# A memory attention and channel mix kernel: all steps put in a new order

## The chip, the cores and the metric

The kernel runs on one core of one Trainium2 chip. The time is device microseconds of that core for one execution of the whole program. Before the change it is 191.7 us (median of 3 runs, 191.69 to 191.99).

## The reference

Two layers, cut to what is computed. For each of 8 batches and 8 heads, 576 tokens of width 64 are first gathered into 32 memory slots, then read back; the result is the input `x` (8 x 576 x 512) of a channel mix.

```python
a = exp(phi - max(phi)); a = a / sum(a)          # over the 576 tokens
k_m = einsum('bhsm,bhsd->bhmd', a, k)            # 32 slots of 64
v_m = einsum('bhsm,bhsd->bhmd', a, v)
attn = softmax(q @ k_m.T / 8)                    # 576 x 32
x = (attn @ v_m) as [B, S, 512]

xk = mu_k * x + (1 - mu_k) * x_prev              # x_prev: the token before
xr = mu_r * x + (1 - mu_r) * x_prev
out = sigmoid(xr @ w_r) * (relu(xk @ w_k) ** 2 @ w_v)
```

## The kernel before, in words

All matrix products are in bf16. The work is cut into steps, and the order of the steps is written out by hand in a list of words, PLAN (lines 19 to 84). A loop at the end of the kernel (lines 794 to 807) takes word after word and issues that step's instructions, so the place of a word in PLAN is the place of its instructions in the queue of each engine that it uses. Nothing reorders them later.

```python
for word in " ".join(PLAN).split():
    word, _, used = word.partition("@")
    word, _, now["by"] = word.partition("/")
    now["banks"] = iter(used)
```

A word is read like this. `2:kv@15` is step `kv` of batch 2, with its PSUM tiles in banks 1 and 5. `/a` or `/d` behind a word says that ScalarE (ACT) or VectorE (DVE) makes the copy. A step that has several parts (matmul, copy, matmul again) stands in the list once for each part.

- `p:k:2` (`preload`, lines 195 to 222) issues the load of k of batch 2 on the queue of GpSimd (POOL); `p:wr`, `p:wv`, `p:wk` load pieces of the weights. k, v and q of two batches fit at a time, phi likewise. A load is cast from f32 to bf16 on its way.
- `exp` makes the exponential of phi on ACT, `z` its sum (matmul with a column of ones, line 329), `kv` the products k_m and v_m (72 small matmuls, line 319). For batch 0 k comes in f32 in two halves and is cast by `c00` to `c11`; its products are `kg0`, `kg1`, those of v `vg0`, `vg1`.
- `nk` scales k_m into `kbd` (line 344 on ACT, 346 on DVE), `tk` transposes it (line 368) and copies it to `kmT` (line 372); `q0`, `q1` transpose q on DVE (line 388); `s` makes the scores (32 small matmuls, line 402), `es0`, `es1` their exponentials; `fe`, `fs`, `fo` the denominators on DVE; `w0`, `w1` the weights `atn` (line 465).
- For batches 1 to 7 x is never made. v_m goes through the weights first: `nv`, `vt` transpose v_m, `G` multiplies it with w_k and w_r (line 492), `E` copies the result to `G` in SBUF (line 498), `D` is a difference of two of those (line 501). Then `c2:5` makes block 5 of 8 of the keys of batch 2: a first part (2 matmuls, line 617), a copy of it into a second PSUM bank (line 621), a second part (4 matmuls, line 625). `g:20` does the same for the gates (lines 679, 683, 687). `r` is the relu (line 583 on ACT, 585 on DVE), `s:25` the square (lines 589, 591), `t` the tanh that stands for the sigmoid (line 656).
- For batch 0 x is made by `mk0`, `mk1`, `mr0`, `mr1` (line 362) and unloaded by `u`; `c0:5a` is a key block of its first half of tokens (line 599), `g:00` to `g:03` are its gates (line 666).
- `o:21` multiplies the squares of one tile of 128 tokens with w_v (8 matmuls, line 757), multiplies with the gate on DVE (line 763) and stores. Names with `a` or `b` take only a part of the 512 columns. `g:e0` to `g:e3` and `o:e0` to `o:e3` do the same for the tokens that are left over from two batches; `x` gathers their squares.
- `mu` and `mub` (lines 260 to 274) put mu_k and mu_r on the partitions, by a transpose and by a broadcast matmul; `m:k0`, `m:k1`, `m:r0` (line 278) scale the weights by them.
- `b:2x8` are 2 matmuls on zeros of 8 x 64 columns (`keep_busy`, line 251); `WARM` is the first row of them, ahead of PLAN.

The loads of POOL are issued in order; an issue waits until the load eight places before it has landed, and until its buffer is free.

Of the kernel before, what the change touches and what calls it, by code (L numbers as in the profile page):

```python
# [85 lines left out]
WARM = (10, 8)  # L86

PRE = "after: id: q:0a"
TAIL = ("o:72", "o:71a", "o:71b",)


NJ = 9
# [5 lines left out]
def kernel(  # L98
# [158 lines left out]

    keep_busy(*WARM)

# [579 lines left out]
```

## Time and profile before

| | |
|---|---|
| median of the runs | 191.7 us |
| the profiled execution | 191.42 us, its span 189.6 us |
| PE busy | 183.6 us, 97% of the span |
| DVE busy | 155.7 us, 82% |
| ACT busy | 153.2 us, 81% |
| POOL busy | 29.5 us, 16% |
| matmuls on zeros | 46, 14.1 us busy |
| moved by DMA | 31.92 MB |

The span runs from the first to the last instruction; the time of an execution has 1.8 us around it. A row of the timeline gives the start, the duration, the engine, the line, the operation, what it writes and reads, and how many; a bracket at its end gives the idle time of the engine before it and what ended that. For a load there are two rows: one with the place and time of its issue, one with the time from the issue to the landing. Matmuls are pipelined, so the busy time of one overlaps with the next: a row's busy time is more than it adds to the chain. In the chain of waits a row is start, duration, engine, tile, line and count.

### The profile page before, as it was taken

How to read it: one execution, taken by the hardware profiler on the slowest of the kernel's cores; microseconds unless marked ns; L12 is line 12 of the kernel's file. 1: busy time of each engine (PE TensorE's matmuls, PEld its weight loads, DVE VectorE, ACT ScalarE, POOL GpSimd, SP SyncE). 2: the span in 40 equal slices, each digit the busy share in tenths (PEclk: the TensorE clock that was granted, in tenths of full speed). 3: DMA queues.
4: the chain of work that ended last, by engine and by line, in shares of the span. 5: the costliest groups of instructions: out<-in, count | busy, mean ns of one | idle time of the engine just before them, and what ended most of it. 6: DMA issues, size and time to landing. Idle time of an engine off the chain costs nothing.

```text
span 189.6 us, 6095 instructions
## 1 busy us (share of the span) xinstructions
PE 183.6 (97%) x2482; PEld 103.4 (55%) x2482; DVE 155.7 (82%) x335; ACT 153.2 (81%) x366; POOL 29.5 (16%) x45
## 2 busy tenths in 40 slices
PE   7999999999999999999999999999999999999991
PEld 2534774768645466556555645655545554465450
DVE  2346887989999999998999998998899998885441
ACT  2646899979999989999999789878898779687800
POOL 5843431041040400510042000000000000000000
PEclk9999999999999999999999999999999999999998
DMA  5999999999999999999939995124304222162064
GB/s 191 279 203 206 269 205 203 255 226 232 295 223 267 257 232 252 303 194 246 225 52 258 231 242 139 31 59 96 75 3 102 63 59 56 25 144 55 2 152 124
DMA packets 25756, 31.92 MB, mean 168 GB/s; under 512 B 2168, under 2 KB 20352, under 8 KB 25728
## 3 DMA queue, kind: packets, MB, share of 16 engines
q0 software_dynamic: 17888, 20.32, 58.1%
q1 hardware_dynamic: 6528, 9.18, 18.4%
q10 hardware_dynamic: 1312, 2.03, 3.0%
q8 instruction: 19, 0.31, 0.6%
q14 instruction: 9, 0.07, 0.1%
HBM read 38.28 MB, written 9.44 MB: 252 GB/s over the span
## 4 chain that ended last, share of the span: by engine, by line
PE 91%; DMA 3%; ACT 3%; DVE 1%; issue 0%; ACTq 0%
PE pv L757 34%; PE pk L617 8%; PE pk L625 8%; PE pb L625 7%; PE gps L492 6%; PE pk L599 4%; PE kvps L319 4%; PE pr L687 3%; PE pr L679 3%; PE pb L687 3%; DMA k0f<-in_k_dram 3%; PE idle L254 2%; PE pr L709 2%; PE pr L666 2%; PE scps L402 2%; PE zps L329 1%
## 5 line engine op out<-in xcount | busy, mean ns | idle before, releaser
L757 PE MATMUL pv<-wv,sq 128*128 128x512 bf16 (+3 forms) x296 | 60.6, 351 | 0.1
L757 PEld LDWEIGHTS <-sq 128*128 128x128 bf16 x296 | 27.9, 98 | 24.4 <-issue 2.1
L498 ACT CAST G<-gps 128x512 bf16<-128x512 f32 x65 | 34.2, 605 | 2.8 <-PE gps L492 2.7
L763 DVE SCALAR_TENSOR_TENSOR o<-sg,pv 128x512 f32<-128x512 f32 (+3 forms) x41 | 25.0, 614 | 7.7 <-PE pv L757 6.5
L625 PEld LDWEIGHTS <-G 128*128 128x128 bf16 x224 | 21.4, 97 | 9.4 <-issue 0.4
L583 ACT ACTIVATE rl<-pk 128x288 bf16<-128x288 f32 (+2 forms) x48 | 19.0, 416 | 6.0 <-PE pk L625 4.4
L625 PE MATMUL pb<-diff,G 128*128 128x288 bf16 x112 | 22.9, 286 | 0.0
L625 PE MATMUL pk<-diff,G 128*128 128x288 bf16 x112 | 22.9, 286 | 0.0
L617 PE MATMUL pk<-atn,G 128*128 128x288 bf16 x112 | 20.2, 286 | 0.0
L589 ACT ACTIVATE sq<-rl 128x576 bf16<-128x576 bf16 (+2 forms) x30 | 18.9, 645 | 0.6 <-DVE rl L585 0.5
L591 DVE TENSOR_TENSOR sq<-rl 128x576 bf16<-128x576 bf16 (+2 forms) x42 | 16.8, 413 | 2.5 <-ACT rl L583 1.8
L621 ACT COPY pb<-pk 128x288 f32<-128x288 f32 x39 | 15.8, 421 | 2.6 <-PE pk L617 2.4
L583 ACT ACTIVATE rl<-pb 128x288 bf16<-128x288 f32 x38 | 15.5, 428 | 2.0 <-PE pb L625 1.8
L254 PE MATMUL idle<-zeros 128*128 128x512 bf16 (+3 forms) x46 | 14.1, 411 | 1.3 <-DVE zeros L180 1.0
L465 DVE TENSOR_TENSOR atn<-e,lz 128x576 bf16<-128x576 bf16 (+2 forms) x18 | 11.9, 681 | 2.9 <-ACT lz L437 2.9
L501 DVE TENSOR_TENSOR G<-G 128x1024 bf16<-128x1024 bf16 x21 | 14.1, 677 | 0.1
L617 PEld LDWEIGHTS <-G 128*128 128x128 bf16 x112 | 10.3, 97 | 6.9 <-issue 1.7
L498 DVE CAST G<-gps 128x512 bf16<-128x512 f32 x19 | 12.4, 679 | 1.4 <-PE gps L492 1.4
L656 ACT ACTIVATE sg<-pr 128x512 f32<-128x512 f32 x22 | 13.0, 613 | 0.0
L388 DVE STREAM_TRANSPOSE qT<-q 128x576 uint32<-128x576 uint32 (+2 forms) x16 | 11.8, 757 | 0.0
L585 DVE TENSOR_SCALAR rl<-pk 128x288 bf16<-128x288 f32 (+2 forms) x24 | 10.4, 445 | 1.0 <-PE pk L625 0.9
L174 POOL DMA_DIRECT2D kv<-in_v_dram x7 | 5.2, 749 | 37.2 <-PE kvps L319 23.0
(100 smaller groups left out, 288.0 us busy)
## 6 DMA issues: line engine op xcount, KB each, us to landing
out_dram<-o SPq DMA_DIRECT2D x53, 128.0 KB, 2.4
q<-in_q_dram POOLq DMA_DIRECT2D x7, 576.0 KB, 14.7
ph<-in_phi_dram POOLq DMA_DIRECT2D x7, 576.0 KB, 15.7
kv<-in_k_dram POOLq DMA_DIRECT2D x7, 576.0 KB, 16.1
kv<-in_v_dram POOLq DMA_DIRECT2D x7, 576.0 KB, 17.4
out_dram<-o SPq DMA_DIRECT2D x28, 64.0 KB, 5.2
k0f<-in_k_dram ACTq DMA_DIRECT2D x2, 576.0 KB, 6.0
wv<-in_moe_w_v_dram POOLq DMA_DIRECT2D x2, 512.0 KB, 18.0
```

What stands on the lines that cost most here:

```text
L254: nc.tensor.matmul(ps.rearrange("p (a b) -> p a b", b=64), lhsT=zeros, rhs=zeros[:, :64].unsqueeze(1).to_broadcast([128, blocks, 64]), sta ...
L498: return lambda: copier()(g_tile()[:, v, c, GCOLS[i]], st["gps", v, i][c])
L501: return lambda: nc.vector.tensor_sub(g_tile()[:, 1, :, GCOLS[i]], g_tile()[:, 2, :, GCOLS[i]], g_tile()[:, 0, :, GCOLS[i]])
L583: nc.scalar.activation(rl, ps, AF.Relu, scale=HALF ** 0.5)
L589: nc.scalar.activation(dst, rl, AF.Square)
L591: nc.vector.tensor_mul(dst, rl, rl)
L617: nc.tensor.matmul(pa, lhsT=st["G"][:, 2, c, f], rhs=st["at"][:, c, :NP], start=c == 0, stop=False, skip_group_check=True)
L621: copier()(pb, pa)
L625: nc.tensor.matmul(ps, lhsT=st["G"][:, v, c, f], rhs=st["d"][:, kind, c], start=False, stop=c == 1, skip_group_check=True)
L656: nc.scalar.activation(gated[name], ps, AF.Tanh, scale=0.5)
L757: nc.tensor.matmul(pv[:, cols], lhsT=squares, rhs=wv_sb[:, fi, cols], start=(fi == 0), stop=(fi == NF - 1))
L763: nc.vector.scalar_tensor_tensor(o[:, cols], in0=gated[name][:, cols], scalar=1.0, in1=pv[:, cols], op0=AL.add, op1=AL.mult)
```

## The change

PLAN is written anew, with the same set of steps. The first row of matmuls on zeros is 17 long instead of 10, and there are 23 instead of 36 in the rest. The broadcast and the transpose of mu stand behind the first scores of batch 0 instead of in front of everything. The pieces of w_k are loaded in another order, and so are the loads from batch 1 on: phi, k, q of batch 1 instead of q, phi, k; q, v, phi, k of batch 2 instead of phi, v, k, q; phi, k, v, q of batch 3 instead of phi, v, k, q. Many copies, relus and squares change between ACT and DVE. The last values stand as 70, 72, e3, 73, 71 instead of 70, 73, e3, 72, 71, and the stores of 72 go out on one queue instead of two. "A rule for the fetch of instructions" is part of how the new order was found; no instruction of the kernel stands for it.

The diff, cut to the rows that hold the front, the steps around kv of batches 2 and 6, and the end:

```diff
-    "0:exp0 0:mu@0 0:mub@1 0:mub 0:c01/a 0:c11/d 0:c00/a 0:exp1 b:11x8@6 b:1x7@6 0:z@1 0:z 0:c10/a 0:kg0@23 0:kg1",
-    "0:mu 0:h0/d 0:h1/d b:2x8@6 b:1x7@6 0:tk@0 0:q0 0:tk b:2x8@6 b:1x7@6 0:s0@0123 p:q:0b p:v:0h p:v:0g 0:q1",
-    "p:wk:0-2 p:wk:4-8 p:wk:2-4 0:es10 0:es00 b:3x8@6 0:l10@4 0:l10 0:l00@5 0:l00 0:r10 0:y10 0:s1@6701 0:es11",
...
-    "c0:0b/d c0:7b/d 1:z c0:6b/d c0:1b/a c0:7b/d x:0/d 0:mr1@1456 1:k@37 0:ur11/d 0:ur10/a b:1x6@2 0:mr0@0215 1:nk/a",
-    "1:tk@3 1:tk 0:ur01/a b:1x8@7 b:1x6@6 1:s@3725 m:k0/d 0:ur00/a 1:es0 1:es1 g:02@0 g:01@1 g:03@2 1:fe 1:fs 0:tb",
-    "g:00@3 o:02b@5 1:fo p:v:2 1:w0 o:03b@7 g:03 g:02 o:02b o:03b o:01b@4 m:r0/a 1:v@60 g:00 p:k:2 p:q:2 g:01",
...
-    "c1:5 c1:7 o:02a r:161/d r:151/a r:150/d r:171/a r:160/d 2:z@4 1:G02@67 r:170/a 2:z 1:Gs2@43 2:kv@15 1:E020/a",
-    "p:q:3 1:Es20/a 2:nk/a s:16/d s:17/d 1:E021/d s:15/d 1:Es21/a o:03a@0 2:tk@4 c1:1/d@6 2:nv/a c1:4@7 o:03a c1:1",
-    "c1:4/a@3 r:111/a 2:vt@0 g:11@1 r:110/a c1:4 2:tk 2:q0 p:phi:4 2:q1 g:10@4 2:vt/a 2:s@0526 r:140/a r:141/a 2:es0",
...
+    "0:exp1 0:c00/d 0:c01/d 0:exp0 b:2x8@7 b:1x6@7 0:kg0@01 p:q:0b 0:z@2 0:z 0:c11/d p:v:0g b:3x8@7 p:v:0h",
+    "p:wk:4-8 p:wk:2-4 0:q0 p:wk:0-2 p:phi:1 p:k:1 p:q:1 p:wr:0-4 p:wv:2-4 0:c10/a p:v:1 0:kg1 0:h0/d 0:h1/a b:4x8@7",
+    "0:tk@0 0:tk 0:q1 b:1x8@7 0:s0@0145 0:mub@3 0:mu@2 0:es00 0:mub 0:mu 0:es10 b:2x8@7 0:l10@2 0:l10 0:l00@3 0:l00 0:r00",
+    "0:y00 0:r10 0:y10 0:vg0@60 0:s1@1452 0:es11 0:es01 b:2x8@3 b:1x7@3 0:vg1 b:1x8@3 0:l01@7 0:nk0 0:l01 0:nk1",
...
+    "p:wv:0-2 c0:4a/a p:q:2 c0:6a@1 c0:4a/a c0:2a@0 0:r11 c0:2a/d c0:7a@2 c0:7a/a c0:3a@4 0:y11 0:mk1@0573 c0:0a@2",
+    "c0:7a/a c0:6a/d p:v:2 c0:2a/d 0:uk11/d c0:1a@1 0:uk10/a c0:7b@0 c0:1b@3 c0:3a/a c0:1a/d c0:3a/a 1:exp c0:6a/d",
...
+    "0:ur00/a 1:q1 p:phi:2 1:nk/a 0:mr1@3567 0:ur11/a 1:tk@0 1:q0 1:tk 0:ur10/a b:2x8@1 1:s@0157 c0:4b/d 1:es1 1:es0",
...
+    "1:Gs1@47 1:Es01/a 1:G00@02 1:d p:k:2 1:Es00/a 1:G01@65 o:01a@3 1:E001/d 1:E010/d 1:E011/a 1:E000/a c1:3@1",
...
+    "p:k:3 p:v:3 1:Gs2@01 1:Es21/a 2:z 1:G02@24 1:E020/a 1:Es20/d 1:E021/d 1:D2 2:kv@53 g:10@6 2:nk/a 2:tk@0 2:tk",
+    "g:11@1 2:nv/a s:16/d g:10/a@2 g:11/d@4 2:s@0357 g:10 g:11 s:15/d 2:es0 2:vt@0 s:14/d 2:es1 3:exp t:101 2:fe",
...
+    "6:nk/a 5:Es21/a 6:q0 6:q1 o:40@3 6:tk@0 5:E020/a 6:nv/a c5:1 r:550/a 6:tk 6:s@0172 r:510/a g:50@4 6:es0 6:vt@5",
...
+    "r:740/a g:70@0 c7:6/d@3 t:710 c7:6 s:74/d c7:7/a@1 g:70/d@7 c7:7 r:770/a r:760/a r:720/d g:70 r:771/a s:72/d",
+    "g:e3 s:77/a r:761/d s:76/d x:7/a t:700 o:70@2 o:72@1 o:70 o:72 o:e3@4 o:73@6 o:e3 o:73 o:71a@0 o:71b@1 t:701",
+    "o:71a o:71b",
 ]
 
-WARM = (10, 8)
+WARM = (17, 8)
 
-TAIL = ("o:72", "o:71a", "o:71b",)
+TAIL = ("o:71a", "o:71b",)
```

105 rows, old and new, of the table PLAN are left out of this document.

## The prediction

> **What bounds the kernel now.** I read the page first, then what TensorE (PE) waited for, then the chain of work that ended last, the timeline of PE, and last the loads one by one, each with its issue and its time to landing.
>
> ```profile
> span 189.6 us, 6095 instructions
> PE 183.6 (97%) x2482; PEld 103.4 (55%) x2482; DVE 155.7 (82%) x335; ACT 153.2 (81%) x366; POOL 29.5 (16%) x45
> DMA  5999999999999999999939995124304222162064
> q8 instruction: 19, 0.31, 0.6%
> ```
>
> ```profile
> PE idle L254 <- DVE zeros L180: 1.0, 1, 1.0
> PE zps L329 <- ACT em L299: 0.2, 1, 0.2
> ```
>
> The second fence is the whole list of waits of PE: 1.0 us before its first instruction and 0.2 us at about 8.5 us. So PE is the bound from 8.5 us to its last matmul at 185.45, and its instruction stream has no stall to be won. The DMA digits matter as much: 9 or more until about 95 us, so the loads form a line that is never empty for half of the kernel.
>
> ```profile
> 18.08 3.31 PE L599 MATMUL pk<-x0T,wk 128*128 128x256 bf16 x28
> 30.11 0.48 PE L402 MATMUL scps<-qT,kmT 32*32 32x288 bf16 x32
> 30.52 1.69 PE L666 MATMUL pr<-wr,x0T 128*128 128x512 bf16 x7
> 48.17 0.84 PE L319 MATMUL kvps<-kv,em 64*32 64x128 bf16 x72
> 52.25 0.48 PE L402 MATMUL scps<-qT,kmT 32*32 32x288 bf16 x32
> 185.45 0.35 DVE o L763
> ```
>
> These are my marks of the timeline: the first key matmul of batch 0 (18.08), the scores of batch 1 (1:s, 30.11), the first gate (30.52), kv of batch 2 (2:kv, 48.17), the scores of batch 2 (2:s, 52.25) and, from the chain, the end of PE.
>
> **The change part by part.** The set of steps is the same in both kernels; only order, banks, fillers and the engine of some copies differ. So the forecast is a comparison of when PE comes to the same mark with the same work behind it.
>
> *Fillers and mu.* The matmuls on zeros go from 46 to 40 (17 instead of 10 in the first row).
>
> ```profile
> 5.37 2.96 PE L254 MATMUL idle<-zeros 128*128 128x512 bf16 x12
> 4.75 0.69 PE L263 MATMUL mub<-mu,sel 8*128 8x128 f32 x4
> 8.45 0.78 DVE L304 CAST kv<-k0f 128x576 bf16<-128x576 f32 x1 [2.22 <-DMA k0f<-in_k_dram]
> ```
>
> The second half of k of batch 0 is in at 8.45 in both kernels, and everything before it is cover: the fillers ahead of it (20 instead of 22) cost nothing. With 17+3 of them PE is done at about 7.0 and idles some 1 us until the casts of k are through; nothing waits for that. The mu broadcast (0.69) and the mu transpose move behind the scores of batch 0, where three fillers of about 0.22 each (from the row of 12) stood in before. DVE's copies of them lie beside the exponentials there. I take 0, with 0.3 as the upper end.
>
> *The front, until 1:s.* Both kernels go through one chain of waits there: kv, kbd, kmT, scores, exponential, logarithm, weights, mixed rows, first key matmul. The new order brings kbd on two engines at once, and v's two products ahead of the second scores instead of behind the second denominators. I get the first key matmul at about 17.6 instead of 18.08, and with 3 fillers instead of 5 behind it 1:s near 29.3 instead of 30.11: a lead of about 0.75, an estimate from 17.6 on: 0.5 there and two fillers (0.4, of which the longer batch-1 chain keeps a part). Its ends are 0 and 0.9: the first gate needs w_r, and in the load line w_r keeps its place.
>
> ```profile
> L201 POOL DMA_DIRECT2D wr<-in_moe_w_r_dram x1: 742/742/742, 12.8 to 12.8; - x1
> DMA to landing us min/median/max: 16.8/16.8/16.8
> ```
>
> 12.8 + 16.8 = 29.6, against 30.52 for the first gate before. The lead's size will matter little: the next part ends it in a wait.
>
> *The load line of batch 2.* This decides the forecast. The loads stand on one queue and land in the order of issue. Before, the order behind the last piece of w_v is phi2, v2, k2, q2, phi3, v3, k3; after, it is q2, v2, phi2, k2, phi3, k3, v3.
>
> ```profile
> L201 POOL DMA_DIRECT2D wv<-in_moe_w_v_dram x1: 886/886/886, 18.9 to 18.9; - x1
> DMA to landing us min/median/max: 19.0/19.0/19.0
> ...
> L174 POOL DMA_DIRECT2D kv<-in_k_dram x1: 740/740/740, 24.8 to 24.8; - x1
> DMA to landing us min/median/max: 21.1/21.1/21.1
> ...
> L174 POOL DMA_DIRECT2D q<-in_q_dram x1: 740/740/740, 27.3 to 27.3; - x1
> DMA to landing us min/median/max: 22.8/22.8/22.8
> ...
> L174 POOL DMA_DIRECT2D kv<-in_k_dram x1: 747/747/747, 38.5 to 38.5; - x1
> DMA to landing us min/median/max: 19.8/19.8/19.8
> ```
>
> Landings before: last w_v 18.9 + 19.0 = 37.9; k2 24.8 + 21.1 = 45.9; q2 27.3 + 22.8 = 50.1; k3 38.5 + 19.8 = 58.3. The four loads of batch 2 took 12.2 us in a line that was full. After, the same four loads follow the same piece of w_v, but k2 is the last of them: it lands at about 50.1, where q2 landed, 4.2 us later than before. And 2:kv needs k2.
>
> When does PE come to 2:kv? Before it, the new order has put one half tile of values, one first and two second parts of keys more than the old one:
>
> ```profile
> 42.07 0.87 PE pv L757 x8
> 86.86 0.25 PE pk L617 x2
> 45.53 0.49 PE pk L617 x4
> 51.89 0.43 PE pr L679 x2
> ```
>
> 0.87 + 0.25 + 2 × 0.49 = 2.1 of work brought forward. So PE comes to 2:kv at 48.17 + 2.1 − 0.75 = 49.5, and waits for k2 until 50.1 or later: 0.6 us and more.
>
> Stores share the line. The old order had put out 7 half tiles of batch 0 (128 KB each) by then, the new one has put out the eighth as well. By bytes, 4 loads of 576 KB and 7 × 128 KB went through in 12.2 us, 0.26 MB per us, so one more store is 0.5 us. [...] Without a rule I take 50.35, between 50.1 (the store finds gaps) and 50.6 (it finds none).
>
> *From 2:kv to 2:s.* The old order had enough work behind 2:kv to hide kbd and kmT. The new one has two first parts of gates (0.43 each). What the chain itself needs is seen at batch 1:
>
> ```profile
> 27.73 0.80 PE L319 MATMUL kvps<-kv,em 64*32 64x64 bf16 x72
> 28.61 0.62 ACT L344 ACTIVATE kbd<-kvps,rz 128x128 bf16<-128x128 f32 x2
> 29.28 0.12 PEld L368 LDWEIGHTS <-kbd 128*128 128x128 bf16 x2 [0.27 <-ACT kbd L344]
> 29.72 0.28 DVE L372 COPY kmT<-ktps 128x256 bf16<-128x256 bf16 x1
> 30.11 0.19 PEld L402 LDWEIGHTS <-kmT 32*32 32x32 bf16 x32 [0.60 <-DVE kmT L372]
> ```
>
> From the start of kv to the weights of the scores: 30.11 − 27.73 = 2.4 us. So 2:s starts at 50.35 + 0.05 + 2.4 = 52.8. At 2:s both kernels have the same work behind them, but for one transpose of v (about 0.1) that the new one still owes: even would be 52.25 − 0.1 = 52.15. Loss 0.65. Ends: with k2 at 50.6, 0.9; with k2 no hindrance, PE at 49.5 gives 51.9, a gain of 0.25.
>
> *Batch 3.* 2:kv to 3:kv holds 7.8 of work in the new order, plus about 0.07 for each change between full and split tiles, so 3:kv comes near 59.2. The seven loads up to v3 are the same set as the seven up to k3 before, 58.3: no second stall, but under 1 us of room.
>
> *Batch 6, the same chain.* Between the transposes of k of batch 6 and its scores stands one second part of keys (0.49 and 0.12 for the transposes), and 30.11 − 29.28 = 0.83 is needed: 0.2 lost, ends 0 and 0.4.
>
> *The end.* After the last key matmul ACT now has three relus, a tanh and a square before the first values of batch 7 can finish:
>
> ```profile
> L583 ACT ACTIVATE rl<-pk 128x288 bf16<-128x288 f32 (+2 forms) x48 | 19.0, 416 | 6.0 <-PE pk L625 4.4
> L589 ACT ACTIVATE sq<-rl 128x576 bf16<-128x576 bf16 (+2 forms) x30 | 18.9, 645 | 0.6 <-DVE rl L585 0.5
> L656 ACT ACTIVATE sg<-pr 128x512 f32<-128x512 f32 x22 | 13.0, 613 | 0.0
> ```
>
> 3 × 0.4 + 0.6 + 0.65 = 2.45 against the gate (2 × 0.43) and seven eighths of a tile of values (1.5), together 2.4: with 0.1 to start, 0.1 lost, ends 0 and 0.5.
>
> *Copies moved between ACT and DVE.* By the steps' marks, 4 casts of G and 6 squares net go to DVE, the scalings of w_k and w_r swap engines. At 0.65 and 0.44 that is about 5 us more for DVE: 161 of 177. It hides behind PE as long as the order keeps DVE level; without that cover it is the third rival.
>
> *The fetch of instructions.* 0.31 MB in 19 packets are 16.3 KB each, and 0.6% of the DMA time; no wait of PE is left over for it. [...] I give the rule 0.
>
> **The sum.** Against the profiled execution, 191.42 us (span 189.6 and 1.8 around it): +0.65 at 2:s, +0.2 at 6:s, +0.1 at the end is 0.95, so 192.4. The runs' median, 191.7, stands 0.28 above that execution: 192.6.
>
> **The rivals.**
> *Even.* PE comes to 2:kv and k2 is just there (it lands by 49.6). Then only the chain to 2:s is left: 0.25 gained, 0.3 lost later, 191.75. For it: 2.3 us of room between k2 and 2:kv before; against: the line's sum of bytes.
> *Faster.* The lead of the front gets through whole. That takes k2 landing before 49.2 and kbd and kmT ready at once, since each us of lateness of k2 is one of PE. 191.7 − 0.75, and the two small losses found covered: 191.0. It decides at k2: 49.2. Against it: a line that is 9 or more in every slice.
> *Slower by more.* DVE or ACT falls behind between 40 and 115 us, where the old order had PE busy without a gap. If each of six batches gives 0.3 away, that is 1.8 on top: 194.4. For it: 5 us more on DVE; against: it had 34 us idle.
> *No fetch wait to remove* is part of the forecast.
>
> **How the numbers follow.** Forecast 0.47 (192.1 to 193.2), even 0.22, faster 0.15, slower by more 0.16. A measurement of this kernel tells about 0.2% (0.4 us) from no change. Faster is the rival's 0.15; within 0.2% (191.3 to 192.1) are the even case and a little of the forecast, 0.24; slower is the rest, 0.61. The range leaves out the ends of the outer rivals: 191.1 to 193.8.
>
> **What would show it.** In the new profile PE should have a wait that the old list lacks: kvps of batch 2 on the DMA of k, 0.5 to 1.1 us, near 50; then kbd and kmT before the scores, some 0.5. 1:s should stand near 29.3 and the first gate not before 29.6. k2's landing should be 50.1 to 50.6. If there is no wait at 2:kv, the order of landing was misread; if 3:kv waits too, the stores weigh more than I give them; if waits spread over batches 3 to 6 with DVE or ACT as releaser, the third rival holds.

## The result, and the profile after

The changed kernel takes 193.39 us (median), the kernel before 191.72: a ratio of 1.0068, with a 95% interval of 1.0045 to 1.0091. It is slower by 0.7%. A time given for a kernel is the median of all its executions, while a ratio leaves out those more than 1.5% above the kernel's fastest (here two at 196.5, at a granted clock of 0.982 and 0.991, against 0.994 to 1.0 in the other six). The profiled execution took 193.23 us, its span is 191.2, against 191.42 and 189.6 before: 1.6 more in the span.

The page of the changed kernel, its first lines:

```profile
span 191.2 us, 6061 instructions
PE 181.0 (95%) x2455; PEld 103.1 (54%) x2476; DVE 161.1 (84%) x341; ACT 148.8 (78%) x360; POOL 29.5 (15%) x45
DMA  5999999999999879999639999222314322422064
```

PE is busy for 2.6 us less, 1.2 of it by fewer zeros (part of the rest are records that the trace lacks: it has 21 matmuls fewer than weight loads), and the span is 1.6 longer. The list of all that PE waited for (engine, tile and line, releaser, then the sum, the times and the longest):

```profile
PE idle L254 <- issue: 1.5, 1, 1.5
PE idle L254 <- DVE zeros L180: 1.0, 1, 1.0
PE ktps L368 <- ACT kbd L344: 0.6, 2, 0.3
PE zps L427 <- DVE mu L274: 0.4, 1, 0.4
PE scps L402 <- DVE kmT L372: 0.3, 2, 0.2
PE ktps L368 <- issue: 0.3, 1, 0.3
PE pv L757 <- issue: 0.2, 1, 0.2
```

The wait of kvps on the DMA of k, on which the forecast stood, is not in it. The largest new one is 1.5 us, put down to "issue": PE waited for nothing that the profile shows, and the instruction behind it is a matmul on zeros, which needs no data. The timeline of PE around it, and at the marks of the prediction:

```profile
14.64 0.59 PE L254 MATMUL idle<-zeros 128*128 128x512 bf16 x2
16.76 0.35 PE L254 MATMUL idle<-zeros 128*128 128x448 bf16 x1 [1.52 <-issue]
17.04 0.45 PE L319 MATMUL kvps<-kv,em 64*32 64x64 bf16 x36
...
19.14 2.90 PE L599 MATMUL pk<-x0T,wk 128*128 128x256 bf16 x24
...
30.94 0.55 PE L402 MATMUL scps<-qT,kmT 32*32 32x288 bf16 x29
...
51.09 0.85 PE L319 MATMUL kvps<-kv,em 64*32 64x128 bf16 x72
...
53.43 0.48 PE L402 MATMUL scps<-qT,kmT 32*32 32x288 bf16 x32 [0.17 <-DVE kmT L372]
...
183.09 3.64 PE L757 MATMUL pv<-wv,sq 128*128 128x512 bf16 x24
```

The last row of the kernel before, for the same 24 matmuls:

```profile
181.78 3.64 PE L757 MATMUL pv<-wv,sq 128*128 128x512 bf16 x24
```

So the loss is there at 1:s already (30.94 against 30.11: 0.83), is 1.28 at 2:s (53.43 against the "even" 52.15) and 1.31 at the last values (183.09 against 181.78). Nothing is lost in the 130 us between. Behind PE's last matmuls the changed kernel needs 191.2 − 186.73 = 4.47 us, the one before 189.6 − 185.42 = 4.18: 0.3 more. That makes the 1.6.

### The profile page after: what moved, and what is told of

It reads as the page before. It is cut to its first block, busy times and chain, and to the rows that moved or that the text cites. A ratio compares the mean times of both kernels' runs of the same rounds, so it can differ in the third digit from the quotient of the medians.

```text
span 191.2 us, 6061 instructions
## 1 busy us (share of the span) xinstructions
PE 181.0 (95%) x2455; PEld 103.1 (54%) x2476; DVE 161.1 (84%) x341; ACT 148.8 (78%) x360; POOL 29.5 (15%) x45
## 4 chain that ended last, share of the span: by engine, by line
PE 87%; ACT 7%; issue 2%; DVE 2%
PE pv L757 30%; PE pk L625 8%; PE pb L625 7%; PE pk L617 7%; PE idle L254 6%; PE gps L492 5%; PE pk L599 4%; ACT G L498 3%; PE kvps L319 3%; PE pb L687 3%; PE pr L679 3%; PE pr L687 3%; PE scps L402 2%; PE pr L666 2%; PE pr L709 2%
## 5 line engine op out<-in xcount | busy, mean ns | idle before, releaser
L757 PE MATMUL pv<-wv,sq 128*128 128x512 bf16 (+3 forms) x282 | 59.3, 349 | 0.8 <-issue 0.2
L498 ACT CAST G<-gps 128x512 bf16<-128x512 f32 x61 | 33.0, 612 | 3.6 <-PE gps L492 3.6
L625 PEld LDWEIGHTS <-G 128*128 128x128 bf16 x224 | 21.5, 98 | 9.1 <-issue 0.8
L583 ACT ACTIVATE rl<-pk 128x288 bf16<-128x288 f32 (+2 forms) x41 | 17.0, 422 | 4.2 <-PE pk L625 1.9
L591 DVE TENSOR_TENSOR sq<-rl 128x576 bf16<-128x576 bf16 (+2 forms) x45 | 18.7, 423 | 1.8 <-ACT rl L583 1.1
L621 ACT COPY pb<-pk 128x288 f32<-128x288 f32 x42 | 16.5, 410 | 3.4 <-PE pk L617 2.6
L589 ACT ACTIVATE sq<-rl 128x576 bf16<-128x576 bf16 (+2 forms) x27 | 16.3, 616 | 0.3 <-DVE rl L585 0.2
L498 DVE CAST G<-gps 128x512 bf16<-128x512 f32 x23 | 15.2, 684 | 0.6 <-PE gps L492 0.5
L254 PE MATMUL idle<-zeros 128*128 128x512 bf16 (+2 forms) x40 | 12.9, 438 | 2.6 <-issue 1.5
L585 DVE TENSOR_SCALAR rl<-pk 128x288 bf16<-128x288 f32 (+2 forms) x31 | 13.4, 441 | 1.6 <-ACT sq L589 1.0
L416 ACT ACTIVATE e<-scps 128x288 bf16<-128x288 f32 x28 | 9.2, 419 | 1.8 <-PE scps L402 1.6
```

The lines of the kernel that those rows point to most:

```text
L254: nc.tensor.matmul(ps.rearrange("p (a b) -> p a b", b=64), lhsT=zeros, rhs=zeros[:, :64].unsqueeze(1).to_broadcast([128, blocks, 64]), sta ...
L498: return lambda: copier()(g_tile()[:, v, c, GCOLS[i]], st["gps", v, i][c])
L583: nc.scalar.activation(rl, ps, AF.Relu, scale=HALF ** 0.5)
L585: nc.vector.tensor_scalar(rl, ps, 0.0, HALF ** 0.5, op0=AL.max, op1=AL.mult)
L589: nc.scalar.activation(dst, rl, AF.Square)
L591: nc.vector.tensor_mul(dst, rl, rl)
```

## The experiments

The theory after the result, called the page theory in what was expected: the stall is the wait for PE's own instructions. They come on DMA queue 8. 19 packets of 16.3 KB hold them, and each shows in the trace; what one packet holds is called a page of instructions. Where a kernel's loads fill the DMA queues (a DMA share of 1.25 to 1.32 of the 16 engines from 8 to 20 us in the changed kernel), a packet can come too late. The rivals: some buffer or transfer is late at that place (data theory); the load line of batch 2 decides, as the forecast had it.

Line numbers of most experiments stand one below those of the changed kernel (L253 for L254), in e8_shift eight above. In the view of the DMA queues a stretch of 0.1 us shows a packet (queue, number, MB, share of the 16 engines). The changed kernel, 14.4 to 14.5 us:

```profile
q8 instruction: 1, 0.02, 60.9%
```

The kernel before, 12.8 to 12.9 us:

```profile
q8 instruction: 1, 0.02, 60.1%
```

These are the first packets of the queue in either trace; by their records they start at 14.46 and 12.86. PE stands still from 15.25 to 16.76 in the one and passes without a stop in the other.

**Is it the count of instructions? 14 rows fewer.**

```diff
-WARM = (17, 8)
+WARM = (10, 8)
```

> The changed kernel with 10 instead of 17 wide matmuls on zeros in the first row: 14 TensorE instructions fewer ahead of everything, nothing else. Page theory: queue 8 carries TensorE's instructions in packets of 16 KB (19 packets, 0.31 MB), 256 instructions each, and the stall of 1.5 us at the matmul on zeros ahead of the second half of v's products of batch 0 is the wait for such a packet. Then the stall moves 14 instructions on, into the 36 matmuls of 0:vg1 (which run without a gap in the changed kernel), with 1.0 to 1.6 us, ending near 16.8; the time stays within 0.4 of the changed kernel. Data theory (a buffer, a bank or a transfer is late at that place): the stall stays at the matmul on zeros, or in front of the first matmul of 0:vg1, and never stands between two matmuls of 0:vg1. Zeros theory (the seven fillers themselves cost time): the stall stays and the time falls by up to 1.5.

Measured: 193.31 us, ratio to the kernel before 1.0077 (1.0049 to 1.0105). The stall stands inside 0:vg1, between two of its 36 matmuls that wait for the same data:

```profile
16.34 0.23 PE L318 MATMUL kvps<-kv,em 64*32 64x64 bf16 x6
17.04 0.41 PE L318 MATMUL kvps<-kv,em 64*32 64x64 bf16 x30 [0.47 <-issue]
```

It moved 14 instructions on, as the page theory said, but it is 0.47 long, not 1.0 to 1.6: with ten zeros the granted clock was 0.50 from 7.65 to 11.06 us, and PE came later to the place. The busy time by stretches counts the instructions ahead of the stall (columns: stretch, its length, busy time and count on PE, PEld, DVE, ACT, POOL, granted clock, DMA share, GB/s). The changed kernel, up to its stall:

```profile
0.00:16.70 16.70, 13.32 (x222) 5.87 (x223) 7.04 (x24) 6.73 (x17) 9.94 (x19) 1.00 1.06 222
```

and the one with ten zeros:

```profile
0.00:17.00 17.00, 13.40 (x222) 5.92 (x223) 6.82 (x24) 6.73 (x17) 9.92 (x19) 0.90 1.06 222
```

222 matmuls and 223 weight loads in both: the 446th instruction waits, whichever it is. (The expectations count four records more, which this view leaves out, and call it row 450.) The same 222 and 223 stand ahead of the stall in e4_chain, e6_wk4, e9_mu, e10_tail and e11_vgh below.

**And 158 rows more.** The edit adds 79 small matmuls on zeros as PE's first work, on top of the cut load of e6_wk4 (next):

```diff
+    keep_small(79)      # 64 x 32 tiles, 64 columns
     keep_busy(*WARM)
```

> The changed kernel with w_k's large load cut in two as before, and 79 small matmuls on zeros (64 x 32, 64 columns) as TensorE's first work: 158 rows more ahead of everything. Page theory: the stall in front of 0:vg1 goes, since row 450 is now some 158 rows earlier, at the mu products and zeros behind the first scores (near 12.0), and its packet is asked for at 6 to 7 us; there the stall is 0 to 0.6. The next page begins 256 rows later, between the second scores' denominators and the first key matmuls; asked for near 12.0, with 3.4 us in the line and 2.35 until it is used, it is ready near 17.8: a stall of 0.2 to 1.0 there. 1:s at 29.2 to 29.9, against 29.84 with the cut load alone. Data theory: the stall of 0.3 to 1.5 stays in front of 0:vg1.

Measured: 201.46 us, ratio 1.0485 (1.0402 to 1.0569). The stall ahead of 0:vg1 is gone, and three others are there:

```profile
18.84 0.31 PE L370 MATMUL mxps<-atn,vm 32*64 32x256 bf16 x7 [0.73 <-issue]
...
34.57 0.36 PE L410 MATMUL scps<-qT,kmT 32*32 32x288 bf16 x15 [2.68 <-issue]
...
61.05 0.28 PE L410 MATMUL scps<-qT,kmT 32*32 32x288 bf16 x1 [2.08 <-issue]
```

```profile
0.00:18.80 18.80, 15.36 (x350) 7.28 (x351) 7.95 (x28) 7.53 (x19) 11.41 (x21) 1.00 1.12 223
0.00:34.50 34.50, 27.95 (x606) 16.23 (x607) 19.84 (x63) 19.11 (x48) 16.78 (x28) 1.00 1.18 221
...
32.00:36.00 4.00, 1.38 (x18) 0.60 (x19) 0.84 (x4) 0.99 (x4) 0.74 (x1) 0.93 1.34 202
36.00:40.00 4.00, 4.00 (x13) 1.55 (x12) 3.57 (x5) 2.76 (x6) 0.00 (x0) 0.65 1.25 207
```

701 and 1213 instructions: 445 + 256 and 445 + 3 × 256. (The third stall has 1977 ahead of it in the trace, four short of 445 + 6 × 256.) So by these counts a page is 256 instructions, and 16.3 KB over 256 is 64 bytes each. The place of the first new stall (0.2 to 1.0 in front of the first key matmuls) was expected; 1:s at 29.2 to 29.9 was not met (31.46), and what the shift does further on was not thought of at all. 0.9 us of small matmuls, in a place where PE has only zeros to do, cost 7.2 us by the medians (201.46 against 194.31 with the cut load alone) and 8.35 between the profiled executions (200.6 and 192.25): 5.5 in three stalls, and some 1.7 by a stretch of 3.4 us behind the second one in which the granted clock was 0.50 (35.41 to 38.83). The rest was not traced; 0.78 of it is a wait for the cast of k. The data theory is out.

What a page needs, from all traces: while the loads keep the queues full, its packet mostly starts 2.2 to 3.9 us after PE has begun the page before it, at the front 3.3 to 3.6. From the packet's start to the first instruction behind a stall it took 2.20 to 2.47 us, in eleven stalls of nine kernels. Together about 5.8, an estimate from the middles of the two, 3.45 and 2.34. In the kernel before, 256 instructions of the front last from 9.4 to 15.4, 6.0: it escapes by 0.2. The changed kernel's last from 9.38 to some 15.25, 5.9, but there the packet took 5.1 us to start. The next five kernels ask why.

**One load cut in two.**

```diff
-p:wk:4-8
+p:wk:4-6 p:wk:6-8
```

> The changed kernel with one load cut in two: blocks 4 to 7 of w_k come as two loads of 256 KB (packets of 512 B) instead of one of 512 KB (packets of 1 KB). TensorE's order is the same. In the changed kernel the first packet of queue 8 starts at 14.4, in the kernel before at 12.8, when a load with short packets (w_k, 256 KB) stands in the line. Line theory (the packet with TensorE's instructions waits behind the loads, longer behind long packets): it starts at 12.8 to 13.5, the stall of 1.5 shrinks to 0 to 0.5, 1:s comes 0.5 to 0.9 earlier and the time falls by as much. Page theory without that (the lateness has nothing to do with what the loads look like): packet near 14.4, stall 1.5, no change. Data theory: the stall stays at 1.5 wherever the packet is.

Measured: the profiled execution 192.25 us; over all executions 194.31 and a ratio of 1.0082 (1.0038 to 1.0125), so that the cut is no cure. In the profiled one, the fastest of twelve, the packet starts at 13.28, as the line theory said, and:

```profile
15.67 0.35 PE L253 MATMUL idle<-zeros 128*128 128x448 bf16 x1 [0.30 <-PE idle L253]
...
29.84 0.56 PE L401 MATMUL scps<-qT,kmT 32*32 32x288 bf16 x32
...
50.00 0.80 PE L318 MATMUL kvps<-kv,em 64*32 64x128 bf16 x72
...
52.33 0.49 PE L401 MATMUL scps<-qT,kmT 32*32 32x288 bf16 x32 [0.17 <-DVE kmT L371]
...
181.98 3.64 PE L756 MATMUL pv<-wv,sq 128*128 128x512 bf16 x24
```

This trace is the changed order with 1.1 us of the stall taken away: 1.10 earlier at 1:s, at 2:s and 1.11 at the last values. So 1.1 of the 1.6 is the late packet, as far as one trace of each kernel can say. That the cut moved the packet is not shown: the other executions of this kernel took 193.2 or more, and two of the changed kernel's own, with the load uncut, took 192.2 and 192.3; none of these has a trace.

**v's halves alone.**

```diff
-p:v:0g ... p:v:0h
+p:v:0h ... p:v:0g
```

> The changed kernel with the two halves of v of batch 0 loaded in the order of the kernel before (second half first); TensorE's order is the same. Question: why the first packet of queue 8 comes 5.1 us after TensorE has begun the page before it in the changed kernel (9.38 to 14.46), when 2.2 to 3.9 us is what all other such packets of the first 60 us show. If the order of v's halves does it: packet at 12.8 to 13.4, stall in front of row 450 of 0 to 0.5, 1:s near 29.9, time 0.8 to 1.1 less than the changed kernel. If not: packet at 14.3 to 14.7, stall 1.4 to 1.9, no change. Data theory: 0:vg0 needs the other half, so it may wait by itself for v, under 0.5.

Measured: packet at 14.46, stall again (14.46 to 16.89 from packet to matmul), 194.93 us, ratio 1.0124 (1.0053 to 1.0195). v's halves alone don't do it.

**The kernel before, with long packets in the line.**

```diff
-p:wk:0-2 p:wk:4-8 p:wk:2-4
+p:wk:0-4 p:wk:4-8
```

> The kernel before with one edit: w_k is loaded in two pieces of 512 KB (packets of 1 KB) instead of three, of which the first had 256 KB (packets of 512 B). TensorE's order is that of the kernel before, which has no stall here. Page theory with the line: in four traces TensorE stood still in front of its row 450 (449 rows before it in order of time), until 2.30 to 2.39 us after the first packet of queue 8 had started; in the kernel before this packet starts at 12.86 and row 450 at 15.37, 2.5 later, so it escapes by 0.1 to 0.2. With long packets in the line the packet should start near 14.5, so a stall of 1.2 to 1.6 us appears in front of row 450, in the first small products of v of batch 0 (15.16 before), and the time rises by 0.8 to 1.3, to 192.5 to 193.0. Data theory: TensorE's order and its data but for w_k are the same, so no stall there; only the first key matmul (18.08) may wait for w_k, by under 0.5.

Measured: 192.26 us, ratio 1.0008 (0.9956 to 1.0060). The packet starts at 13.36, not at 14.5, and there is no stall at the place; a weight load of the first key products waits 0.36 for w_k. The size of the packets ahead, on which the expectation stood, wasn't enough here to make the packet late.

**The kernel before, w_k's pieces in the new order.**

```diff
-p:wk:0-2 p:wk:4-8 p:wk:2-4
+p:wk:4-8 p:wk:2-4 p:wk:0-2
```

> The kernel before with the pieces of w_k loaded in the order of the changed kernel (blocks 4 to 7 first, then 2 and 3, then 0 and 1). Blocks 0 and 1 are what its first key products need, so these wait until about 20 and the time rises by 1.5 to 2.5; this run is for the front ahead of them. If the order of w_k's pieces makes the packet late: it starts at 14.3 to 14.7 instead of 12.86, and a stall of 1.2 to 1.6 us stands in front of row 450 (15.38 before). If not: packet at 12.7 to 13.5, no stall there.

Measured: packet at 13.03, no stall there; 193.13 us, ratio 1.005 (1.001 to 1.009). The wait that was expected accounts for it:

```profile
PE pk L599 <- DMA wk<-in_moe_w_k_dram: 2.0, 1, 2.0
```

**All loads of the front in the old order, under the new order of PE.**

```diff
-p:v:0g p:v:0h  p:wk:4-8 p:wk:2-4 p:wk:0-2  p:phi:1 p:k:1 p:q:1
+p:v:0h p:v:0g  p:wk:0-2 p:wk:4-8 p:wk:2-4  p:q:1 p:phi:1 p:k:1
```

> The changed kernel with all loads of the front in the order of the kernel before: v's second half first, w_k's blocks 0 and 1, then 4 to 7, then 2 and 3, and q, phi, k of batch 1. TensorE's order is that of the changed kernel. So far the first packet of queue 8 started at 12.7 to 13.4 in the four kernels with the old front, and at 14.4 to 15.0 in the six with the new front and its three loads of w_k; v's halves alone and w_k's pieces alone did not move it. Line theory (the loads of the front, all together, set it): 12.7 to 13.4 here, stall in front of row 450 of 0 to 0.4, time 191.8 to 192.6, with a new wait of up to 1.0 of the first key matmul for w_k's blocks 4 to 7, which land near 18.7. The other theory (TensorE's own order and the time at which it gets to the page before set it): 14.3 to 15.0 again, stall of 1.4 to 1.9, time 193.2 or more.

Measured: packet at 13.15, no wait for instructions. By these traces the loads of the front set the packet's start, all together: 12.72 to 13.36 in the five traces with the old loads, this one among them, and 14.40 to 14.95 in the six with the new loads uncut (v's halves exchanged in one of them). The time at which PE began the page before doesn't part the two groups: 9.28 to 9.77 in the five, 9.24 to 10.36 in the six. Each kernel has one trace. The time that was expected was missed, 194.43 (ratio 1.0122, 1.0058 to 1.0185): the first products of v now wait for a half of v that lands late.

```profile
15.21 0.44 PE L318 MATMUL kvps<-kv,em 64*32 64x64 bf16 x36 [1.28 <-DMA kv<-in_v_dram]
```

```profile
12.64:16.05 3.41, 1.76 (x73) 0.87 (x72) 1.69 (x5) 1.92 (x6) 1.33 (x2) 1.00 1.32 203
16.05:19.46 3.41, 3.35 (x58) 1.13 (x56) 1.13 (x4) 1.45 (x6) 1.79 (x3) 0.50 1.32 206
```

With this wait and 0.38 at mu, PE was idle for 1.65 of 3.41 us, and in the 3.41 us behind them the granted clock was 0.50. So the new order as it stands needs its own loads, and with these the instructions come late. Which pair of loads it is stays open.

**mu back in front** (with the cut load).

```diff
-... 0:s0@0145 0:mub@3 0:mu@2 0:es00 0:mub 0:mu ...
+b:1x6@7 0:mu@2 0:mub@3 0:mub 0:mu 0:kg0@01 ...  0:s0@0145 0:es00 ...
```

> The changed kernel with w_k's large load cut in two, and the broadcast and the transpose of mu put back among the first zeros, ahead of the first products of k. My forecast priced the place of mu at 0, at most 0.3; the trace of the changed kernel shows a wait of 0.38 for mu's copy behind the first scores. Page theory: that wait goes, but TensorE only comes earlier to row 450 and waits there for the same packet, 0.4 longer: 1:s stays within 0.15 of 29.84, and the time does not change. Data theory (mu's wait is on the path by itself): 1:s comes 0.3 to 0.4 earlier, near 29.45, and the time falls as much.

Measured: 193.25 us, ratio 1.0101 (1.0074 to 1.0128). Neither came: 1:s is at 30.56, 0.7 later than with the cut load alone.

```profile
9.64 0.36 PE L328 MATMUL zps<-ones,em 128*128 128x2 bf16 x9 [0.54 <-DVE mu L273]
...
13.98 0.43 PE L426 MATMUL zps<-e,sumh 128*128 128x320 bf16 x2 [0.54 <-ACT e L419]
...
16.40 0.35 PE L253 MATMUL idle<-zeros 128*128 128x448 bf16 x1 [0.68 <-PE idle L253]
```

In front the copies of mu stand on DVE ahead of what the sums need, 0.54; the wait behind the scores stays, now for an exponential; and PE begins the page before only at 10.76, so the packet (14.20) is late again. In these two traces the place behind the scores is the better one; over all executions the two kernels can't be told apart (ratios 1.0101 here, 1.0082 there), and what the place costs by itself can't be told from this.

**The loads of batches 2 and 3 in the old order.**

```diff
-p:q:2 p:v:2 p:phi:2 p:k:2  p:phi:3 p:k:3 p:v:3 p:q:3
+p:phi:2 p:v:2 p:k:2 p:q:2  p:phi:3 p:v:3 p:k:3 p:q:3
```

> The changed kernel with the loads of batches 2 and 3 in the order of the kernel before (phi, v, k, q each), at the changed kernel's places in the queue. My forecast's load-line step: k of batch 2 is last of four and lands late, so that 2:kv waits 0.5 to 1.1; with the old order k is the third, lands some 4 us earlier, and 0.3 to 0.65 us come back. By the trace of the changed kernel (k of batch 2 lands at 48.9, 2:kv starts at 51.1 without a wait) nothing comes back: time and all marks within 0.2, unless the packet in the front comes at another time. A rival: q or another load of batch 2 or 3 is now late, and a new wait of under 0.5 stands at its transposes.

Measured: 201.58 us, ratio 1.048 (1.0402 to 1.0558). 3.2 of the 8 are there at 1:s (34.17), from a stall for instructions that ends at 17.39 and a granted clock of 0.50 from 16.94 to 23.76. From 1:s to 2:kv it then takes 24.06, 3.9 more than the changed kernel's 20.15:

```profile
49.10 0.78 DVE L387 STREAM_TRANSPOSE qT<-q 128x576 uint32<-128x576 uint32 x1 [2.82 <-DMA q<-in_q_dram]
...
50.60 0.41 PE L616 MATMUL pk<-atn,G 128*128 128x288 bf16 x2 [2.19 <-DVE o L762]
```

The wait of 2.19 and another 3.41 us at a clock of 0.50 (51.07 to 54.48), worth 1.7, make up the 3.9. The new order of steps transposes q of batch 2 early, so q has to be first in the line and k can be last. The rival in the expectation held, at several times its size. Giving k its old place gave nothing back, but with so much lost elsewhere this run is no clean test of it; what refutes the forecast's reading of the load line is the landing of k in the trace of the changed kernel (below).

**The old front under the new rest.**

```diff
-the words up to 1:s of the changed order, WARM = (17, 8)
+the words up to 1:s of the kernel before, WARM = (10, 8); behind them the changed order, banks renamed
```

> The front of the kernel before (all words up to the scores of batch 1, its 10 zeros in front, its loads, mu ahead), and behind it the changed order with its banks renamed. Front theory: all that the changed kernel loses until the scores of batch 1 (0.8 to 0.9 us) is made in the front, so 1:s starts near 30.1 again, no stall of over 0.5 us stands before it, and the time is 0.6 to 1.0 less than the changed kernel, 192.4 to 192.8. My forecast's theory: the load line of batch 2 decides; then PE, which comes to 2:kv near 50.2 here, waits there for k of batch 2 until 50.1 to 50.6, and up to 0.5 of the gain is lost again. By the trace of the changed kernel k of batch 2 lands at 48.9, so that I expect no wait there.

Measured: no stall in the front, 1:s at 29.95, packet at 12.72.

```profile
38.02 0.23 PE L470 MATMUL vtps<-identity,vb 128*128 128x128 bf16 x1 [0.40 <-ACT vb L353]
50.63 0.81 PE L319 MATMUL kvps<-kv,em 64*32 64x128 bf16 x72
52.97 0.33 PE L402 MATMUL scps<-qT,kmT 32*32 32x288 bf16 x9 [0.17 <-DVE kmT L372]
```

The front gives back the 1.0 at 1:s, and 2:kv doesn't wait for k though PE is there 0.5 earlier. But half of the gain is gone at 2:s (0.46), 0.40 of it in a new wait at the transposes of v, and the end stands 5.0 us behind PE. At the last values it is 182.62, 0.84 behind the kernel before, with no stall for instructions. The profiled execution took 193.12 and the six 193.1 to 196.1 (median 195.58, ratio 1.0142, 1.0078 to 1.0205); what the longer ones lost no trace shows. The time that was expected, 192.4 to 192.8, was missed, and against the changed kernel the run is inconclusive.

**Cover for the chain of batch 2.**

```diff
-c1:7 r:170/d o:02a@5 ... c1:6/d@6 o:02a ... 2:kv@53 g:10@6 2:nk/a 2:tk@0 2:tk g:11@1
+... 2:kv@53 2:nk/a o:02a@7 2:tk@0 2:tk g:10@6 g:11@1 ... 2:s@0357 o:02a
```

> The changed kernel with half a tile of values (o:02a, 4 matmuls, 0.87 us) moved from ahead of 2:kv to between 2:kv and 2:tk, one first part of a gate from ahead of 2:tk to behind it, and 2:exp somewhat earlier. My forecast's step for the chain from 2:kv to 2:s says that this stretch lacks cover: then the waits at the transposes of k (0.28) and at the scores (0.17) of batch 2 go, and 0.3 to 0.4 us of the time with them. Rival: the 0.35 that the changed kernel loses between 2:kv and 2:s is only a shift of work between marks; then the time stays within 0.2. k theory: 2:kv now comes 0.9 earlier, near 50.2, against a landing of k of batch 2 at 48.9: no wait; if k lands after 50.2, the gain is eaten.

Measured: 196.32 us, ratio 1.018 (1.0116 to 1.0245), a failure:

```profile
PE pk L624 <- DVE pb L620: 1.1, 1, 1.1
PE scps L401 <- DVE o L762: 0.9, 1, 0.9
```

The half tile of values needs DVE, which is late there, and holds bank 7, which the scores need. This says nothing of the chain's own price. The run shows something else. Its stall for instructions is 1.66 long, not 1.52, and then:

```profile
15.11:18.53 3.42, 1.76 (x57) 0.74 (x55) 1.71 (x6) 1.41 (x8) 0.75 (x1) 1.00 1.38 222
18.53:21.94 3.41, 3.41 (x29) 1.91 (x14) 2.58 (x9) 2.26 (x7) 1.83 (x3) 0.50 1.15 270
```

The changed kernel's profiled execution, in the stretch of its own stall and the one behind it:

```profile
15.35:18.76 3.41, 2.00 (x58) 0.93 (x58) 1.87 (x7) 1.54 (x8) 0.76 (x2) 1.00 1.39 234
18.76:22.17 3.41, 3.41 (x48) 2.58 (x54) 3.05 (x10) 2.48 (x9) 2.00 (x3) 1.00 1.16 260
```

For 3.41 us the granted clock is 0.50, where the changed kernel had 1.00. PE was busy all that time, so half a clock costs half of 3.41, 1.7, and 1:s comes at 32.59, 1.65 later than there. That is the second price of the late packet in this trace.

**The stores at the end.**

```diff
-TAIL = ("o:71a", "o:71b",)
+TAIL = ("o:72", "o:71a", "o:71b",)
```

> The changed kernel, with the stores of the values 72 on two queues again, as before the change. The changed kernel's span ends 4.45 us after TensorE's last matmuls, the kernel before's 4.15. My forecast's step for the end put 0.1 there, for other reasons. If the stores on one queue cost it: the end comes 4.1 to 4.2 behind TensorE and the time falls by 0.3. If not (the last stores, 71, decide): 4.4 to 4.6, no change. The front is that of the changed kernel: the packet should start at 14.3 to 14.7 again with a stall of 1.4 to 1.9.

Measured: 194.58 us, ratio 1.005 (0.9995 to 1.0105). The front stalled as expected (packet 14.40, stall 1.65), and a clock of 0.50 from 18.55 to 21.96 made PE later still; both lie long before the end, which is what this run is for:

```profile
span 192.9 us, 6083 instructions
```

```profile
184.62 3.64 PE L756 MATMUL pv<-wv,sq 128*128 128x512 bf16 x24
```

192.9 − 188.26 = 4.64 behind PE: the queues of those stores are not the 0.3. What is, stays open.

No kernel of these runs is faster than the kernel before.

## Why the prediction was right, and where it was wrong

The direction was right (slower, 192.6 forecast, 193.4 measured), and the time lies inside the whole range of 191.1 to 193.8, though above the 192.1 to 193.2 that the forecast gave its own mechanism. Most of the reason was wrong: of the terms 0.65, 0.2 and 0.1, only a part of the first is in the trace, and the largest loss was in a step priced at 0. That the number came near is luck.

- *The fetch of instructions*, "no wait of PE is left over for it ... I give the rule 0": this step failed. It costs 1.1 us in the profiled execution (the changed kernel against e6_wk4, at every mark) and more where the clock falls (another 1.65 at 1:s in e4_chain). The trace of before had shown 0 truly, but by 0.2 us of room, and a change of order with 256 other instructions between 9.4 and 15.4 us, behind other loads, has to be checked for that room anew. In the runs the stalls for instructions are 0.30 (e6_wk4) to 2.68 us (e8_shift) long.
- *The front, until 1:s*, a lead of 0.75, between 0 and 0.9: failed in sign, 0.83 late, by the same packet. With most of the stall away (the trace of e6_wk4) the lead is 0.27; there 0.30 of a wait remains at the zeros and 0.38 at mu.
- *Fillers and mu*, 0 with 0.3 as the upper end: the wait behind the scores is 0.38 long. PE isn't done with the zeros at 7.0, with 1 us to spare, but at 7.8, and goes straight on to k's products. Ten zeros instead (e1_warm10) leave PE idle for 1.6 us at the casts of k, and the granted clock is 0.50 from 7.65 to 11.06.
- *The load line of batch 2*: failed. k landed at 27.44 + 21.5 = 48.9, not 50.35:

```profile
L174 POOL DMA_DIRECT2D kv<-in_k_dram x1: 742/742/742, 27.4 to 27.4; - x1
DMA to landing us min/median/max: 21.5/21.5/21.5
```

  and 2:kv (51.09; 50.00 in e6_wk4) had nothing to wait for. What failed is the time for the line: the four loads behind the last piece of w_v took 11.3 us (37.65 to 48.94), not 12.2 and a store's share. No run shows the 0.25 to 0.5 that the store was to add: k landed 1.2 ahead of 50.1. PE was also 1.6 later than forecast, by the front, but at the forecast's own 49.5 it would not have waited either.
- *From 2:kv to 2:s*, a chain of 2.4: right, 51.09 to 53.43 is 2.34. What is lost there, counted from 1:s to 2:s, is 1.28 − 0.83 = 0.45, and the same in e6_wk4 (0.27 + 0.18). The forecast's 0.65 there had the wait for k in it.
- *Batch 3*: right that 3:kv (59.55) waits for no load; the room is larger than the 1 us given, since k of batch 3 is issued at 32.7 and lands 21.7 later, at 54.4. The 0.07 for a change from full to split tiles is 0.09 in the trace of before: 0.31 from a 128x512 matmul at 59.81 to the 64*32 tiles behind it at 60.12, and 0.22 from one such matmul to the next (51.72 to 52.25 for two and the change, 0.53).
- *Batch 6* and *The end*, 0.2 and 0.1: neither shows ahead of PE's end (1.28 at 2:s, 1.31 at the last values). Behind it 0.3 was lost for a reason that wasn't found.
- *Copies moved*: right. DVE has 161.1 us, and from 2:s on the loss stays flat. The rival with DVE falling behind would have shown there.
- Of the rivals, *Even* had the better account of the order by itself: taking the two stalls for instructions (1.1 and 0.30) off the 1.31 at the last values leaves the new order within 0.1 of the old one there. This is worked out, not run, and e2_oldfront, the new order from 1:s on without a stall for instructions, is 0.84 behind there under the old front.

## What to carry to other kernels

Count TensorE's instructions before you move steps. Here the first one of a page of 256 waited (instruction 446 in eight kernels, 702 and 1214 in e8_shift) for a packet that shares the DMA engines with the loads: from 14.4 to 14.5 us of the changed kernel the trace has 20 packets of the loads and this one. In this kernel 256 instructions had to last about 5.8 us, by the estimate above, while the loads were running. Stretches of small matmuls make a page short: 36 of them took 0.45 us in the changed kernel (17.04), 24 of 128x256 took 2.90 (19.14). Instructions added or removed ahead shifted the later pages: 14 fewer moved the stall 14 on (e1_warm10), 158 more put three others in its place (e8_shift), so an edit "in idle time" can cost more than the work it adds: 7.2 us there for 0.9. A wait on "issue" in front of an instruction that needs no data was the sign (1.52 at 16.76 in the changed kernel), and the packets of the instruction queue stand in the trace beside it (14.46).

## What was not expected of the hardware

- 79 small matmuls, 0.87 us of busy time, cost 7 to 8 us (e8_shift), 5.5 of it in three stalls that come from shifting the pages.
- The start of a page's packet went with the loads: in the traces mostly 2.2 to 3.9 us after PE has begun the page before it in the first 60 us, at most 1.5 us beyond 115 us, where the last loads land (the changed kernel issues its last at 102). In six kernels the first one took 4.3 to 5.3.
- The granted clock fell to 0.50 for stretches of 3.41 us (one of them twice as long), and what came before a fall was idle time in one wait (1.65 in e10_tail) or in several (1.12 and most of 0.45 in e1_warm10). In the fourteen traces there are eight falls while PE was at work; in the 3.41 us ahead of each, PE was idle for 1.47 to 2.62 us. Behind the stretches with 1.41 or less none came, behind two others, with 1.59 and 1.75, none either. Where no fall shows a border, it is an estimate, in steps of 3.413 from a fall of the same trace (3.413: the two falls of e3_loads begin at 16.94 and 51.07, ten steps apart).
- These stretches begin at different times in the traces (15.35 in the changed kernel, 15.11 in e4_chain, 15.14 in e10_tail), and that may have decided. The stall of 1.52 in the changed kernel began 0.1 us ahead of a border (15.35, 51 steps before 189.43, where the clock falls behind PE's last work) and left 1.41 of idle time in the stretch: no fall. The stall of 1.65 in e10_tail lay whole in one (15.14 to 18.55): a fall.
